# Moving the sums of batch 0 to VectorE, hT in two signs, and small writes to GpSimd in an attention kernel on one core

## The chip, the cores and the metric

The kernel runs on one core of a Trainium2 chip. The metric is the device time of one execution in microseconds (us). Engines are named as in the profile: PE is TensorE (PEld its weight loads), DVE is VectorE, ACT is ScalarE, POOL is GpSimd, SP is SyncE.

## What is computed

Two small networks one after the other. With x of 4 batches x 12544 rows x 128, and 32 inducing rows:

```python
def mab(q, kv):
    s = scale * (q @ kv.transpose(0, 2, 1))
    s = s - s.max(-1, keepdims=True)
    a = np.exp(s)
    a /= a.sum(-1, keepdims=True) + 1e-09
    return a @ kv
h = mab(I, x)            # 32 x 128 for each batch
y = mab(x, h)            # 12544 x 128 for each batch
...
h1 = y @ w1              # 128 x 1024
h2 = y @ w2
g = np.maximum(h1, h2)
return (g @ w_out)       # 1024 x 128
```

The kernel uses max(h1, h2) = relu(h2 - h1) + h1. So the output is relu(e (h (w2 - w1))) w_out + e (h w1 w_out), divided by the sums of e, where e are the exponentials of the second attention.

## The kernel before, in words

**Head: first attention of batch 0.** The x of batch 0 comes in 11 parts of 14, 7, 6, 5 or 3 slabs (a slab is 128 rows). Part 0 is loaded over SyncE's queue as fp32 and cast; parts 1 to 10 are loaded by GpSimd's queue with a cast to fp16 (load_x, L165). After them in the same queue come w1, w2 and w_out (L210 to L212), a memset of the tile m1bd (L219), seven loads of batch 1 (L165), and the four fp32 loads of weights_1 (L516, L517). For each part, p1_transpose has TensorE transpose the slabs (L232) and VectorE (L236) and ScalarE (L239) copy the result; p1_scores multiplies them with the inducing rows (L248) and ScalarE takes exponentials, et (L257); p1_accum has TensorE form the sums of et (L271, one column each) and the 32 x 128 sum h (L280). Between them, L657 and L665 are matmuls that compute nothing (fill).

**Ramp.** small_h scales h into hT (L423) and copies the sums (L433). weights_2 transposes w1 (L530). small_sums spreads the sums over the partitions with one fp32 matmul (L449) and takes the reciprocals rs and rw (L453, L454). stage computes e for a block of tokens (L591 on TensorE, L603 on ScalarE). small_hwd computes hwd = h (w2 - w1) (L469 and L470; copies at L477 and L484). weights_3 computes w1 w_out (L543, L551). small_m1 computes m1 = h w1 w_out (L493) and writes it to m1 and, as a diagonal block, to m1bd (L500 for batch 0, L504 for batch 3).

**Main loop.** A phase is four row-tiled matmul groups, e times hwd (L990, or m1 times e); ScalarE (L1006) and VectorE (L1009) take the relu of it out of PSUM. Output matmuls multiply the relu with w_out (L809). The first group of batch 0 and the last block of batch 3 are finished instead by a matmul with m1bd (L786). VectorE then divides by the sums of e (L836) and SyncE writes the output (L861). SyncE's queue also holds the DMA transposes of the next batch's x (L171). L766 are matmuls that compute nothing, put where the planner expects TensorE to wait.

**What sets the order.** All five engines are scheduled by hand: each engine's instruction order is the order in which the Python program emits them. The program decides what to emit next with a clock of its own (class Clock: expected times of TensorE, ScalarE, VectorE and of each of the eight PSUM banks; there is none for GpSimd) and with a table DEV, which tells for certain steps of the loop to deviate from the rule.

The program between the head and the loop ends like this:

```python
phase(plan_phase(False))
weights_3()
phase(plan_phase(False))
pending.append((small_m1, (0,)))
state["stage"] = 2
weights_1b()
```

weights_1b (L522) has GpSimd subtract the fp32 weights of weights_1 for the later batches (w21, first read at 92.8 us). small_m1 waits in the list pending and is emitted in the loop that follows.

Of the kernel before, what the change touches and what calls it, by code (L numbers as in the profile page):

```python
# [102 lines left out]
def kernel(  # L103
# [24 lines left out]
    etp = ctx.enter_context(tc.tile_pool(name="etp", bufs=3))  # L128
# [10 lines left out]
    ck = Clock()  # L139
    uid = [0]  # L140
# [37 lines left out]
    ones32 = consts.tile([128, 128], F32, name="ones32")  # L178
# [13 lines left out]
    rep32 = consts.tile([128, 128], F32, name="rep32")  # L192
# [4 lines left out]
    with tc.manual_schedule(engines={ET.PE, ET.DVE, ET.Activation, ET.Pool, ET.SP}):  # L197
# [5 lines left out]
        nc.sync.dma_start(ind_sb, inducing)  # L203
# [7 lines left out]
        nc.gpsimd.dma_start(out=w2h, in_=moe_w2)  # L211
# [3 lines left out]
        nc.vector.memset(ones32, 1.0)  # L215
# [7 lines left out]
        def p1_transpose(b, i, between=0):  # L223
# [3 lines left out]
            for g, m in ((0, h), (h, n - h)):  # L227
                if g and between:
                    fill(between)
                bi, ps = bank([128, 8, 128], F16)  # L230
                for j in range(m):
                    nc.tensor.transpose(ps[:, j, :], xn[:, g + j, :], identity16)  # L232
                end = ck.run(0.056 * m, ready=ck.bank[bi], why="T")
                dst = xT_tiles[b % 2][:, k0 + g : k0 + g + m, :]
                if g == 0:
                    nc.vector.tensor_copy(out=dst, in_=ps[:, 0:m, :])  # L236
                    ck.bank[bi] = ck.on_dve(end, 0.08 + 0.075 * m)
                else:
                    nc.scalar.copy(out=dst, in_=ps[:, 0:m, :])  # L239
                    ck.bank[bi] = ck.on_act(end, 0.05 + 0.12 * m)  # L240
                st[b]["xT", i] = max(ck.bank[bi], st[b].get(("xT", i), 0.0))
# [18 lines left out]

        def p1_accum(b, i, lo=0, hi=P1):
# [4 lines left out]
            if b == 0:  # L266
                last = i == len(parts[0]) - 1
                ck.wait(ready, "p1")
                for j in range(lo, hi, 4):
                    m = min(4, hi - j)  # L270
                    nc.tensor.matmul(  # L271
                        out=st[0]["eps"][0 : m * M, 0:1],
                        lhsT=et[:, j : j + m, :].rearrange("p k m -> p (k m)"),
                        rhs=ones16[:, 0:1],
                        start=(i == 0 and j == 0),
                        stop=(last and j + m == n),
                        skip_group_check=True,
                    )
# [8 lines left out]
                st[0]["end"] = ck.run(0.029 * (hi - lo) + 0.03 * ((hi - lo + 3) // 4))  # L287
# [130 lines left out]
        def small_h(b):  # L418
            hT4 = smp.tile([C, 4, M], F16, name=f"hT4_{b}", tag="hT4")
            if b == 0:  # L420


                nc.vector.tensor_scalar(  # L423
                    out=hT4,
                    in0=st[0]["hps"][:, None, 0:M].broadcast_to((C, 4, M)),
                    scalar1=DOWN,
# [3 lines left out]
                st[b]["hT4r"] = ck.on_dve(st[0]["end"], 0.3)  # L430
                ck.bank[st[0]["hb"]] = st[b]["hT4r"]
                es = smp.tile([128, 1], F32, name="es_0", tag="es")
                nc.scalar.copy(out=es, in_=st[0]["eps"][:, 0:1])  # L433
                ready = ck.on_act(st[0]["end"], 0.2)
                st[b]["hT4"] = hT4.rearrange("c q m -> c (q m)")
                return es, ready
# [8 lines left out]
        def small_sums(es, ready):  # L445

            ps = st[0]["eps"]
            ck.wait(ready, "p1")
            nc.tensor.matmul(out=ps[:, 2:3], lhsT=rep32, rhs=es, start=True, stop=True, skip_group_check=True)  # L449
            end = ck.run(0.11)  # L450
            st[0]["rs"] = smp.tile([128, 1], F32, name="rs_0", tag="rs_")
            st[0]["rw"] = smp.tile([128, 1], F32, name="rw_0", tag="rw_")
            nc.vector.reciprocal(out=st[0]["rs"], in_=ps[:, 2:3])  # L453
            nc.vector.tensor_scalar(out=st[0]["rw"], in0=st[0]["rs"], scalar1=1.0 / scale, scalar2=None, op0=ALU.mult)  # L454
            ck.bank[st[0]["eb"]] = st[0]["rsr"] = ck.on_dve(end, 0.34)

        def small_hwd(b, halves=(0, 1)):
            if 0 in halves:
                st[b]["hwd"] = smp.tile([128, J], F16, name=f"hwd_{b}", tag="hwd")
            hwd = st[b]["hwd"]  # L460
            for half in halves:
                for n in range(2 if b == 0 and half == 0 else 1):
# [5 lines left out]
                    if b == 0:  # L468
                        nc.tensor.matmul(out=ps, lhsT=st[b]["hT4"], rhs=w2h[:, sl], start=True, stop=False)  # L469
                        nc.tensor.matmul(out=ps, lhsT=st[b]["hT4"], rhs=w1h[:, sl], start=False, stop=True)  # L470
# [4 lines left out]
                    if half == 0 and n == 0:  # L475
# [14 lines left out]
        def small_m1(b):  # L490
            bi, ps = bank([128, 512])
            ck.wait(max(ck.bank[bi], st[b]["hT4r"]), "p1")
# [4 lines left out]
            outs = [(m1bd[32 * q : 32 * (q + 1), q, :], slice(32 * q, 32 * (q + 1))) for q in bd]  # L497
            for o, r in outs + [(m1, slice(0, 128))]:
                if b == 0:
                    nc.vector.tensor_scalar(  # L500
                        out=o, in0=ps[r, 0:128], scalar1=st[0]["rw"][r, :], scalar2=None, op0=ALU.mult
                    )
                else:
                    nc.vector.tensor_copy(out=o, in_=ps[r, 0:128])  # L504
                ck.bank[bi] = ck.on_dve(end, 0.2)
# [3 lines left out]
        w_of = {}  # L509

# [13 lines left out]
        def weights_2():  # L524
            for g in range(2):
                bi, ps = bank([128, 4, 128], F16)
                ck.wait(ck.bank[bi], "w")
# [3 lines left out]
                end = ck.run(0.056 * 4)  # L531
                if g == 0:
                    nc.vector.tensor_copy(out=w1T[:, 0:4, :], in_=ps)
                    ck.bank[bi] = ck.on_dve(end, 0.4)
                else:
                    nc.scalar.copy(out=w1T[:, 4:8, :], in_=ps)
                    ck.bank[bi] = w_of["w1T"] = ck.on_act(end, 0.5)

        def weights_3():
            bi, ps = bank([128, 512])  # L540
            ck.wait(max(ck.bank[bi], w_of["w1T"]), "w")
# [9 lines left out]
            nc.scalar.mul(out=w1out, in_=ps[:, 0:128], mul=-1.0)  # L551
            ck.bank[bi] = w_of["w1out"] = ck.on_act(end, 0.2)
# [73 lines left out]
        def dens(blk):  # L626
# [6 lines left out]
            bi, ps = bank([128, 512])  # L633
            ck.wait(ck.bank[bi], "den bank")
# [17 lines left out]
            ck.bank[bi] = ck.on_dve(end, 0.18 + 0.001 * 4 * n)  # L652
# [16 lines left out]
        for i in range(4):  # L669
            p1_transpose(0, i, 2 if i == 0 else 0)  # L670
            if i < 3:
                fill(2 - i // 2)
            if i == 0:
                bi, ps = bank([128, 512])
                nc.tensor.transpose(ps[:, 0:M], ind_sb, identity32[0:M, 0:M])
                nc.vector.tensor_copy(out=inducingT, in_=ps[:, 0:M])
                ck.bank[bi] = 0.0
                nc.vector.reduce_sum(out=diag, in_=identity32.rearrange("p (k m) -> p m k", m=M), axis=AX.X)
                for dst, f in ((rep32, DOWN / scale), (repd, 1.0)):
                    nc.vector.tensor_scalar(  # L680
                        out=dst.rearrange("p (k m) -> p k m", m=M),
                        in0=diag[:, None, :].broadcast_to((128, 4, M)),
                        scalar1=f,
                        scalar2=None,
                        op0=ALU.mult,
                    )
            if i > 0:
                p1_accum(0, i - 1)
            p1_scores(0, i)
        last = len(parts[0]) - 1  # L690
        p1_transpose(0, 4)
        p1_accum(0, 3)
        p1_transpose(0, 5)
        p1_scores(0, 4)
        for i in range(6, last + 1):
            p1_transpose(0, i)
            p1_scores(0, i - 1)
            p1_accum(0, i - 2)
        p1_scores(0, last)
        p1_accum(0, last - 1)  # L700
        p1_accum(0, last)
        for i in range(7):
            load_x(1, i)
        weights_1()
        nc.vector.tensor_scalar(out=w1h, in0=w1h, scalar1=-1.0, scalar2=None, op0=ALU.mult)
        sums = small_h(0)
        weights_2()
        small_sums(*sums)
        stage(blocks[0])
        small_hwd(0, (0,))  # L710
# [26 lines left out]
        def final_ready():  # L737
# [14 lines left out]
            return r  # L752
# [25 lines left out]
        def linear_last(end):  # L778

            while held:  # L780
                g = held[0]
                if g.full:
                    if st[g.blk.b].get("m1r", INF) > ck.pe:
# [102 lines left out]
        def want_linear():  # L886
# [7 lines left out]
            if st[g.blk.b].get("m1r", 0.0) > ck.pe + 0.2:  # L894
# [7 lines left out]
            22: 2, 33: 2, 78: 1, 95: 1, 97: 1, 103: 1, 104: 1, 106: 4, 116: 1, 118: 1, 119: 1, 125: 1, 127:  # L902
            2, 130: 1, 133: 1, 149: 2, 155: 1, 157: 4, 172: 1, 200: 1, 219: 1, 256: 2, 268: 1, 276: 3, 285:
            2, 297: 1, 324: 1, 327: 1, 339: 1, 344: 1, 357: 1, 368: 1, 399: 1, 466: 1, 478: 4, 481: 1, 484:
            1, 497: 1, 510: 2, 564: 1, 580: 1, 616: 2, 638: 1, 674: 4, 679: 1, 688: 1, 700: 3, 725: 2, 771:
            1, 784: 2, 795: 1, 830: 1, 832: 1, 838: 3, 839: 1, 847: 2, 855: 4, 932: 2, 958: 1, 962: 1, 969:
            1, 974: 1, 979: 1, 981: 1, 1041: 3, 1075: 1, 1102: 1, 1141: 4, 1154: 1, 1162: 2, 1168: 4, 1174:
            1, 1181: 2, 1207: 2, 1241: 1, 1247: 1, 1254: 1, 1258: 1, 1295: 1, 1331: 3, 1332: 3, 1343: 4,
            1365: 2, 1367: 1, 1380: 1, 1386: 1, 1390: 4, 1407: 4, 1411: 4, 1413: 3, 1420: 1, 1434: 1, 1442:
# [295 lines left out]
```

## Time and profile before

| what | us |
|---|---|
| median of 3 runs | 327.37 (327.37 to 327.51) |
| span of the profiled execution, first to last instruction | 325.6 |
| around the span (median less span) | 1.77 |
| first phase (L990) starts | 24.29 |
| first matmul with m1bd (L786) starts | 29.75 |
| m1bd written by VectorE (L500) | 27.38, takes 0.25 |
| subtractions of the weights by GpSimd (L522) | 41.11 and 42.54, 1.27 each |
| first output written out (L861) | 31.10 |

The profiled execution's own whole time is not recorded apart from the runs; its span is set against their median. A row of a timeline has the start, the length from the first start to the last end, engine, line, operation, out<-in and the count; in brackets the idle time of the engine before it and what ended that. A row of the chain has start, length and work. Matmul ends in the profile are modelled, so a busy TensorE is not one at its peak. The matmuls that compute nothing count as busy.

### The profile page before, as it was taken

Reading aid. Unit: us, or ns where it says so; the run is one execution under the profiler, and the core shown is the slowest. Engines: PE = TensorE matmul, PEld = TensorE weight load, DVE = VectorE, ACT = ScalarE, POOL = GpSimd, SP = SyncE. Lnnn points to the kernel's source line nnn. Section 1 sums busy time; section 2 is a strip of 40 time slices with the busy share of each in tenths; the row PEclk is TensorE's granted clock in tenths of the full one; section 3 lists DMA queues with packets and bytes.
Section 4 is the critical chain, followed back from the end, with each engine's and each line's share of the span. In section 5 each row is a group of like instructions: output and inputs, shape, how many; then the busy total and the mean of one; then the engine's idle time right before and its main releaser. Section 6 shows DMA issues by size and latency. Waiting matters only on the chain.

```text
span 325.6 us, 12570 instructions
## 1 busy us (share of the span) xinstructions
PE 319.8 (98%) x5404; PEld 243.0 (75%) x5404; DVE 283.1 (87%) x509; ACT 281.7 (87%) x560; POOL 25.6 (8%) x51
## 2 busy tenths in 40 slices
PE   7999999999999999999999999999999999999996
PEld 3876777777767777777777777777777777778785
DVE  3359989989989998998989999998989999999973
ACT  3679899999989899998888999989969999999961
POOL 7452030000040000000040000000000000000000
PEclk9999999999999999999999999999999999999999
DMA  8999999976279999993389999992312312222233
GB/s 204 208 206 214 286 246 212 172 207 134 97 150 245 225 248 209 201 203 86 116 162 243 214 234 232 190 192 86 115 66 101 113 68 98 90 108 99 85 115 112
DMA packets 70823, 53.65 MB, mean 165 GB/s; under 512 B 52176, under 2 KB 55408, under 8 KB 70768
## 3 DMA queue, kind: packets, MB, share of 16 engines
q1 hardware_dynamic: 64656, 38.63, 49.2%
q0 software_dynamic: 6112, 14.22, 22.3%
q8 instruction: 42, 0.69, 0.9%
q14 instruction: 13, 0.11, 0.1%
HBM read 28.33 MB, written 25.69 MB: 166 GB/s over the span
## 4 chain that ended last, share of the span: by engine, by line
PE 95%; DVE 1%; DMA 1%; ACT 0%; issue 0%; ACTq 0%; DVEq 0%
PE ps L809 61%; PE ps L990 22%; PE ps L591 2%; PE ps L232 2%; PE ps L308 2%; PE ps L364 1%; DMA xf<-in_x_dram 1%; PE ps L248 1%; DVE relu L1009 1%; PE ps L280 1%; PE ps L641 1%; PE ps L766 1%; PE ps L271 1%; PE ps L657 0%; PE ps L473 0%; PE ps L409 0%
## 5 line engine op out<-in xcount | busy, mean ns | idle before, releaser
L1006 ACT ACTIVATE relu<-ps 128x512 f16<-128x512 f32 x461 | 244.8, 602 | 26.6 <-PE ps L990 18.1
L1009 DVE TENSOR_SCALAR relu<-ps 128x512 f16<-128x512 f32 x323 | 206.8, 682 | 16.9 <-PE ps L990 15.3
L809 PE MATMUL ps<-woutp,relu 128*128 128x128 f16 x3136 | 217.3, 220 | 0.0
L809 PEld LDWEIGHTS <-relu 128*128 128x128 f16 x3136 | 176.7, 98 | 39.6 <-issue 29.1
L990 PE MATMUL ps<-e,hwd 32*128 32x512 f16 (+2 forms) x880 | 88.7, 360 | 0.0
L836 DVE TENSOR_TENSOR o<-ps,rp 128x512 f32<-128x512 f32 (+3 forms) x108 | 68.5, 634 | 5.5 <-PE ps L809 3.4
L990 PEld LDWEIGHTS <-hwd 32*128 32x128 f16 x880 | 24.9, 91 | 21.1 <-issue 1.0
L990 PE MATMUL ps<-m,e 32*128 32x128 f16 x381 | 38.8, 217 | 0.0
L990 PEld LDWEIGHTS <-e 32*128 32x128 f16 x381 | 21.3, 93 | 2.6
L165 POOL DMA_DIRECT2D xn<-in_x_dram x31 | 17.0, 557 | 8.2 <-DMA xn<-in_x_dram 4.3
L236 DVE COPY xT<-ps 128x512 f16<-128x512 f16 (+3 forms) x11 | 5.5, 504 | 7.8 <-PE ps L232 7.7
L319 ACT ACTIVATE eu<-ps 128x512 f16<-128x512 f32 x18 | 10.8, 615 | 0.0
L603 ACT ACTIVATE e<-ps 128x512 f16<-128x512 f32 (+2 forms) x21 | 10.5, 577 | 0.0
L164 POOL COPY pace<-hacc 128x1 f32<-128x1 f32 x2 | 0.4, 184 | 114.8 <-DVE hacc L397 114.8
L591 PE MATMUL ps<-xT,hT 128*32 128x512 f16 (+3 forms) x114 | 8.9, 362 | 0.0
L239 ACT COPY xT<-ps 128x768 f16<-128x768 f16 (+3 forms) x11 | 6.1, 556 | 2.7 <-PE ps L232 2.6
L232 PE MATMUL ps<-identity,xn 128*128 128x128 f16 x98 | 7.4, 219 | 0.4 <-DVE xn L661 0.3
L232 PEld LDWEIGHTS <-xn 128*128 128x128 f16 x98 | 5.6, 97 | 1.6 <-DVE xn L661 1.1
L257 ACT ACTIVATE et<-ps 128x448 f16<-128x448 f32 (+4 forms) x11 | 4.5, 413 | 2.6 <-PE ps L248 2.6
L308 PE MATMUL ps<-xT,inducingT 128*32 128x512 f16 x72 | 6.5, 385 | 0.0
L591 PEld LDWEIGHTS <-hT 128*32 128x32 f16 x114 | 3.3, 94 | 4.1 <-issue 3.0
L364 PE MATMUL ps<-xn,eT 128*32 128x128 f16 x288 | 5.5, 220 | 0.0
(96 smaller groups left out, 108.2 us busy)
## 6 DMA issues: line engine op xcount, KB each, us to landing
out_dram<-o SPq DMA_DIRECT2D x90, 256.0 KB, 2.4
xn<-in_x_dram POOLq DMA_DIRECT2D x24, 448.0 KB, 11.8
out_dram<-o SPq DMA_DIRECT2D x10, 128.0 KB, 3.0
xn<-in_moe_w_dram POOLq DMA_DIRECT2D x4, 256.0 KB, 14.1
xn<-in_x_dram POOLq DMA_DIRECT2D x4, 224.0 KB, 10.2
xT<-xn SPq DMA_TRANSPOSE x42, 4.3
xf<-in_x_dram SPq DMA_DIRECT2D x1, 512.0 KB, 3.9
xf<-in_x_dram SPq DMA_DIRECT2D x1, 384.0 KB, 4.3
```

The costliest lines, as they stand in the source:

```text
L165: nc.gpsimd.dma_start(out=xn_at[b, i][:, 0:n, :], in_=xr[b, :, k0 : k0 + n, :])
L232: nc.tensor.transpose(ps[:, j, :], xn[:, g + j, :], identity16)
L308: nc.tensor.matmul(out=ps[32 * g : 32 * (g + 1), :], lhsT=inducingT, rhs=xT_tiles[b % 2][:, U * u + 4 * g : U * u + 4 * (g + 1), :], start ...
L319: nc.scalar.activation(out=eu, in_=ps, func=AF.Exp, scale=scale, accum_out=st[b]["es"][:, u : u + 1])
L364: nc.tensor.matmul(out=ps[32 * g : 32 * (g + 1), 0:128], lhsT=eT[:, j, 32 * g : 32 * (g + 1)], rhs=xn_of(b, U * v + 4 * g + j), start=(j = ...
L591: nc.tensor.matmul(out=ps[32 * q : 32 * (q + 1), 128 * t : 128 * (t + n)], lhsT=hq, rhs=xT[:, c : c + n, :], start=True, stop=True, tile_p ...
L603: nc.scalar.activation(out=blk.e2[:, 0 : 128 * wd], in_=ps[:, 0 : 128 * wd], func=AF.Exp, scale=st[0]["rs"] if blk.b == 0 else scale,)
L809: nc.tensor.matmul(out=g.ps[:, 128 * c : 128 * (c + 1)], lhsT=g.blk.relu[q][:, 128 * (jb * w4 + t) : 128 * (jb * w4 + t + 1)], rhs=woutp[: ...
L836: nc.vector.tensor_mul(osb[:, 0:n, :], g.ps[:, 0 : n * C].rearrange("p (s c) -> p s c", s=n), rp)
L990: nc.tensor.matmul(**seq[i])
L1006: nc.scalar.activation(out=dst, in_=src, func=AF.Relu)
L1009: nc.vector.tensor_scalar(out=dst, in0=src, scalar1=0.0, scalar2=None, op0=ALU.max)
```

## The change

- The one-column matmuls of p1_accum (L271) go. A new function p1_sum has VectorE reduce et over the slabs of each part, add the parts up, and repeat the last sum four times; small_sums multiplies that with a column of the constant DOWN in one fp32 matmul. et gets four buffers instead of three.
- hT is copied by ScalarE, and a negated copy by VectorE; w1 is no longer negated. The product with w1 reads the negated copy. w1 w_out is copied without a sign.
- Both 256-column pieces of hwd are copied by VectorE; the first comes before the first stage, the second behind it.
- m1bd is no longer written by VectorE from PSUM: GpSimd copies it from m1.
- inducing is loaded over ScalarE's queue and transposed before x; w2 comes in two halves; one fill matmul less at two places; the order of the parts' steps changes; three small results share a PSUM bank (misc).
- The planner's clock starts at 1.2 us, knows when loads land (LANDED), and two entries of DEV differ. w1 w_out stands behind the first phase in the instruction order of both kernels.

The core of the diff:

```diff
-        nc.sync.dma_start(ind_sb, inducing)
+        nc.scalar.dma_start(ind_sb, inducing)
...
-        nc.gpsimd.dma_start(out=w2h, in_=moe_w2)
+        for h in range(2):
+            sl = slice(512 * h, 512 * (h + 1))
+            nc.gpsimd.dma_start(out=w2h[:, sl], in_=moe_w2[:, sl])
...
+        def p1_sum(i):
+            k0, n = parts[0][i]
+            et, ready = st[0]["et", i]
+            part = esum
+            if i > 0:
+                part = smp.tile([128, M], F32, name=f"esum_{i}", tag="esp")
+            nc.vector.reduce_sum(out=part, in_=et[:, 0:n, :].rearrange("p k m -> p m k"), axis=AX.X)
+            st[0]["sum"] = ck.on_dve(ready, 0.08 + n * M / 960.0)
+            if i == len(parts[0]) - 1:
+                nc.vector.tensor_add(
+                    out=esum4,
+                    in0=esum[:, None, :].broadcast_to((128, 4, M)),
+                    in1=part[:, None, :].broadcast_to((128, 4, M)),
+                )
+                st[0]["sum"] = ck.on_dve(0.0, 0.2)
+            elif i > 0:
+                nc.vector.tensor_add(out=esum, in0=part, in1=esum)
+                ck.on_dve(0.0, 0.1)
...
-                for j in range(lo, hi, 4):
-                    m = min(4, hi - j)
-                    nc.tensor.matmul(
-                        out=st[0]["eps"][0 : m * M, 0:1],
-                        lhsT=et[:, j : j + m, :].rearrange("p k m -> p (k m)"),
-                        rhs=ones16[:, 0:1],
...
+                nc.scalar.activation(
+                    out=hT4,
+                    in_=st[0]["hps"][:, None, 0:M].broadcast_to((C, 4, M)),
+                    func=AF.Copy,
+                    scale=DOWN,
+                )
...
+                neg = smp.tile([C, 4, M], F16, name="hT4n_0", tag="hT4n")
                 nc.vector.tensor_scalar(
-                    out=hT4,
+                    out=neg,
                     in0=st[0]["hps"][:, None, 0:M].broadcast_to((C, 4, M)),
-                    scalar1=DOWN,
+                    scalar1=-DOWN,
...
-            nc.tensor.matmul(out=ps[:, 2:3], lhsT=rep32, rhs=es, start=True, stop=True, skip_group_check=True)
+            nc.tensor.matmul(
+                out=ps[:, 0:1], lhsT=esum4.rearrange("p q m -> p (q m)"), rhs=down32, start=True, stop=True
+            )
...
         def small_m1(b):
-            bi, ps = bank([128, 512])
+            bi, ps = misc(256) if b == 0 else bank([128, 512])
...
-            outs = [(m1bd[32 * q : 32 * (q + 1), q, :], slice(32 * q, 32 * (q + 1))) for q in bd]
-            for o, r in outs + [(m1, slice(0, 128))]:
-                if b == 0:
-                    nc.vector.tensor_scalar(
-                        out=o, in0=ps[r, 0:128], scalar1=st[0]["rw"][r, :], scalar2=None, op0=ALU.mult
-                    )
-                else:
-                    nc.vector.tensor_copy(out=o, in_=ps[r, 0:128])
-                ck.bank[bi] = ck.on_dve(end, 0.2)
+            if b == 0:
+                nc.vector.tensor_scalar(out=m1, in0=ps[:, 0:128], scalar1=st[0]["rw"], scalar2=None, op0=ALU.mult)
+            else:
+                nc.vector.tensor_copy(out=m1, in_=ps[:, 0:128])
+            ck.bank[bi] = ck.on_dve(end, 0.2)
+            for q in bd:
+                r = slice(32 * q, 32 * (q + 1))
+                nc.gpsimd.tensor_copy(out=m1bd[r, q, :], in_=m1[r, :])
+            st[b]["m1bdr"] = ck.bank[bi] + 0.5 + 0.3 * len(bd)
...
+        def misc(lo):
+            if "misc" not in w_of:
+                w_of["misc"] = bank([128, 512])
+                ck.wait(ck.bank[w_of["misc"][0]], "misc")
+                ck.bank[w_of["misc"][0]] = INF
+            bi, ps = w_of["misc"]
+            return bi, ps[:, lo : lo + 128]
...
-            nc.scalar.mul(out=w1out, in_=ps[:, 0:128], mul=-1.0)
+            nc.scalar.copy(out=w1out, in_=ps[:, 0:128])
...
         last = len(parts[0]) - 1
...
+        for i in range(2, last):
+            if i > 2:
+                p1_sum(i - 3)
             p1_transpose(0, i)
             p1_scores(0, i - 1)
-            p1_accum(0, i - 2)
+            if i < last - 1:
+                p1_accum(0, i - 2)
...
-        nc.vector.tensor_scalar(out=w1h, in0=w1h, scalar1=-1.0, scalar2=None, op0=ALU.mult)
-        sums = small_h(0)
+        small_h(0)
         weights_2()
-        small_sums(*sums)
+        small_sums()
+        small_hwd(0, (0,), (0,))
         stage(blocks[0])
-        small_hwd(0, (0,))
+        small_hwd(0, (0,), (1,))
...
                 if g.full:
-                    if st[g.blk.b].get("m1r", INF) > ck.pe:
+                    if st[g.blk.b].get("m1bdr", INF) > ck.pe:
                         return
...
         phase(plan_phase(False))
-        weights_3()
+        blocks[0].staged = max(blocks[0].staged, st[0]["hwdr"])
+        weights_3(0)
         phase(plan_phase(False))
```

## The prediction

> **What bounds the kernel.** I read the page first (busy shares, slices, chain), then the timelines of TensorE and GpSimd for 0 to 45 us, then the waits.
>
> ```profile
> PE 319.8 (98%) x5404; PEld 243.0 (75%) x5404; DVE 283.1 (87%) x509; ACT 281.7 (87%) x560; POOL 25.6 (8%) x51
> ...
> PE 95%; DVE 1%; DMA 1%; ACT 0%; issue 0%; ACTq 0%; DVEq 0%
> ```
>
> TensorE is busy for 98% of the span, and 95% of the chain that ended last is TensorE's own work. So a microsecond that TensorE loses anywhere after the ramp is a microsecond of the result, unless something later gives it back. GpSimd looks free (8%), which is the trap in this case: the share says nothing of how long its queue stands still.
>
> The ramp ends near 29.7 us. From there the chain in order of time is TensorE piece after TensorE piece without a gap:
>
> ```profile
> 29.72 0.19 PE ps L809
> 29.91 0.06 PE ps L786
> 29.96 0.56 PE ps L809 x10
> 30.52 0.28 PE ps L990 x3
> 30.80 0.71 PE ps L809 x10
> ```
>
> L786 is the matmul that finishes the first output group; its moving operand is m1bd. In the timeline of TensorE it starts at 29.75 us. Now the timeline of GpSimd (start, length, what; in brackets the idle time before it and what ended it):
>
> ```profile
> 14.52 0.89 POOL L212 DMA_DIRECT2D woutp<-in_moe_w_out_dram  x1 [0.57 <-DMA xn<-in_x_dram]
> 15.40 0.54 POOL L219 MEMSET m1bd<- 128x512 f16 x1
> ...
> 26.14 0.54 POOL L517 DMA_DIRECT2D xn<-in_moe_w_dram  x1 [1.61 <-PE ps L641]
> 28.34 0.54 POOL L516 DMA_DIRECT2D xn<-in_moe_w_dram  x1 [1.66 <-DMA xn<-in_x_dram]
> 30.45 0.54 POOL L517 DMA_DIRECT2D xn<-in_moe_w_dram  x1 [1.57 <-PE ps L786]
> 41.11 1.27 POOL L522 TENSOR_TENSOR w<-xn,xn 128x512 f16<-128x512 f32 x1 [10.12 <-DMA xn<-in_moe_w_dram]
> 42.54 1.27 POOL L522 TENSOR_TENSOR w<-xn,xn 128x512 f16<-128x512 f32 x1 [0.15 <-DMA xn<-in_moe_w_dram]
> ```
>
> The two L522 are weights_1b's subtractions w2 - w1. GpSimd stands 10.12 us before the first, because the four fp32 weight loads are behind seven loads of batch 1, and is through with them at 42.54 + 1.27 = 43.81 us. In this kernel nobody cares: w21 is first read at 92.8 us.
>
> **The change, part by part.**
>
> *m1bd on GpSimd (the part that decides).* VectorE wrote the block of m1bd at 27.38 (L500, 0.25 us) straight from PSUM. In the changed kernel GpSimd copies it from m1. small_m1 runs inside the main loop, and weights_1b() is called ahead of that loop, so in GpSimd's instruction order the copy stands right behind both subtractions: load, load, load, load, subtract, subtract, copy to m1bd. TensorE's order still has the m1bd matmul after the fifth phase, with a wait on GpSimd in front of it. So a wait is added, and what is queued behind it is all the rest of TensorE's program. VectorE's next output (the first L836, at 30.80) needs that matmul, and SyncE's first output and all its transposes (31.10, 34.83 and on) stand behind that output. No engine can feed TensorE in the meantime.
>
> Does GpSimd keep its order? The memset of m1bd above waits for nothing, and still ran only at 15.40, behind five DMA issues that GpSimd stood waiting to make, for 0.97, 1.62, 1.67, 0.54 and 0.57 us from 7.0 on. It doesn't let a ready instruction pass a waiting one.
>
> When is the copy done? Upper figure: the subtractions as now, to 43.81; a gap of 0.1; the copy, 32x128, between the 0.18 of the 128x1 copy (L164) and the 0.54 of the 128x512 memset: I take 0.3; TensorE starts 0.07 after its releaser (VectorE's first cast ends at 5.31, the transposes start at 5.38). That is 44.3. Lower figure: SyncE's outputs and transposes between 31 and 42.5 us won't be there. The issues at 26.14, 28.34, 30.45 each wait for one more landing of a 448 KB load, so the queue alone lands one in 2.15 us. Four more from 30.45 make 39.05 in issue times, less 0.3 between a landing and the issue behind it, 38.75; the four weight loads at 1.43 a pair (42.54 - 41.11) end at 41.6; subtraction 42.9, copy and signal 43.35. Splitting w2 adds one DMA to the queue for the same bytes, so I allow 0.1 and take **43.5**, near the lower end because the competing transfers are surely gone. Delay of the m1bd matmul against now: 43.5 - 29.75 = **13.75 us**, bounds 13.6 and 14.55.
>
> *TensorE after the standstill.* The only place in this trace where TensorE comes out of idleness is the start:
>
> ```profile
> 1.19 3.85 PE L665 MATMUL ps<-warm 128*128 128x512 f16 x9 [1.19 <-DVE warm L213]
> ...
> 5.83 0.60 PE L657 MATMUL ps<-warm 128*128 128x512 f16 x2
> ```
>
> Nine 128x512 matmuls take 3.85 us, 0.43 each; the two at 5.83 take 0.45 together in the chain, 0.22 each. The granted clock reads 1.00 in both, so the page doesn't show it. If 13 us of idleness bring that state back, 9 x 0.21 = **1.9 us** more are lost (0 if they don't; 2.1 if the half rate lasted to the first transposes: (5.38 - 1.19) / 2). TensorE has no slack afterwards to hide it. The row doesn't tell how long an idle time it needs; I take 1.9, from the one case there is.
>
> [...]
>
> *Sums of batch 0 by VectorE.* 29 one-column matmuls (L271) go, four in 0.27 us at 9.58: 29 x 0.066 = 1.9 us of TensorE between 9.6 and 21.6. VectorE gets 11 reductions, 9 adds and one broadcast add: the nearest row is the 128x128 reduction L678, 0.36, so 21 x 0.15 to 0.7, some 3 to 15 us, and I take 8, in a stretch where it is busy 2.4 of 5 us. The transposes of the last part of x start at 20.01, issued 10.16 and landed 9.3 later, at 19.5: at most 0.55 is to be won there. Against it, the last reductions, the broadcast add, the negated hT and the w1T copy (0.42) now stand in VectorE's queue before the reciprocal that the first exponentials need; that can cost as much as it wins.
>
> *hT plain and negated, weights, order.* The negation of w1h (0.43), one copy of es (0.16) and the diag scaling (0.28) go; the hT copy moves to ScalarE (a 128x128 there: L551, 0.30), the negated one to VectorE (0.29 now); the second 256-column hwd piece moves from ScalarE to VectorE (0.48). The fp32 sum matmul keeps its form (0.34). 14 instead of 16 fill matmuls of 512 columns, 12 instead of 13 of 256. inducing is loaded over ScalarE's queue, and its transpose now stands ahead of x's first: if it still landed at 1.66 + 5.2 = 6.9, the first transposes would slip 1.5 us. w1 times w_out stands behind the first phase in both instruction orders; only its PSUM bank and sign change. Three small results now share one bank.
>
> **All of this head is worth between -1.0 (0.55, and the 0.43 of the negation, which now stands between the last copies and hT) and +2.0 us (the slip of 1.5, and 0.5 in VectorE's queue) at the first phase (24.29 now). I take -0.3, and none of it counts:** whatever it wins, TensorE then waits longer for the same copy, whose time comes from GpSimd's load queue; whatever it costs is covered up to 13 us. Without that cover it would be the whole result.
>
> *The rest.* After the m1bd matmul the two instruction orders of TensorE agree until about two thirds of the program, then phases and output matmuls change places with equal counts: -0.4 to +0.4, taken as 0. The last batch's four m1bd copies leave VectorE (4 x 0.29 at 242 to 243) for an idle GpSimd, and are needed near 320: nothing.
>
> **Sum.** Span 325.6, plus 1.77 around it, is the median 327.37. 325.6 + 13.75 + 1.9 = 341.25 span, **343.0 us**.
>
> **Rivals.** (a) The standstill without the half rate: 327.37 + 13.75 = 341.1. For it: no row shows an idle time in mid-run that brings it back; against: the start. 0.16. (b) No standstill: the copy runs before TensorE arrives at 29.75, so only the head counts, 327.37 - 0.3 = 327.1, from 326.4 (head 1 faster) to 329.4. It needs the copy past the subtractions, or the weights landed by 29.75 - 0.47 - 2 x 1.27 = 26.7 instead of 42.5; it decides once that margin of 16 us is gone. Against it stand the order, the 10.12 and the memset. 0.04: half of it faster, a quarter same, a quarter slower. (c) The loads land as late as now or later, 44.3 and beyond, with the half rate: 327.37 + 14.55 + 1.9 = 343.8 and up. 0.18. The forecast, resume at 43.3 to 43.9 with the half rate: 0.62.
>
> The range takes in (a) at its lower bound, 13.6, with 0.4 less from the reordering: 340.6. It takes in (c) with 0.2 more of half rate, 0.4 of reordering and 0.3 of later loads: 344.7. What a measurement of this kernel can tell from no change is about 0.2%, 0.65 us. Faster 0.02, same 0.01, slower 0.97.
>
> **What would show it.** Right: GpSimd's m1bd copy right after the second subtraction, near 43 us; TensorE idle from about 29.5 to 43.5, put down to GpSimd; no output before 43; the first 128x128 matmuls after it at 0.11 instead of 0.056 for some 4 us (wrong about the half rate if at 0.056 at once). Wrong altogether: a copy before 30 us. Wrong in size: subtractions before 41 or after 43 us.

## The result and the profile after

The changed kernel takes 342.58 us (median of 5 runs, 342.17 to 343.17) against 327.48 for the kernel before: 1.0464 times as long, interval 1.0451 to 1.0476. The forecast was 343.0. The span is 340.6 us, 15.0 more than before.

On the page of the changed kernel, the busy shares, the slices of TensorE and its granted clock, and the chain by engine:

```profile
PE 321.6 (94%) x5372; PEld 243.1 (71%) x5372; DVE 290.0 (85%) x525; ACT 281.4 (83%) x558; POOL 27.3 (8%) x57
...
PE   8878099999999999999999999999999999999996
...
PEclk9989679999999999999999999999999999999999
...
PE 87%; DMA 6%; DVE 3%; POOL 1%; issue 1%; POOLq 0%
```

GpSimd still shows 8%. The fifth slice of TensorE (34 to 42.6 us) is a 0, and the clock is below full speed in two places: around 25 us and around 37 to 47 us (the digits 8, and 6 and 7; by windows it is 0.50 from 23.5 to 26.9 and from 37.1 to 47.4). Loads have grown from 1% to 6% of the chain (4% of it the fp32 weight loads), and GpSimd has come into it. The timelines of GpSimd and of TensorE in the changed kernel:

```profile
30.40 0.54 POOL L552 DMA_DIRECT2D xn<-in_moe_w_dram  x1 [1.62 <-PE ps L846]
40.00 2.51 POOL L557 TENSOR_TENSOR w<-xn,xn 128x512 f16<-128x512 f32 x2 [9.06 <-DMA xn<-in_moe_w_dram]
42.45 0.28 POOL L531 COPY m1bd<-m 32x128 f16<-32x128 f16 x1
```

```profile
32.89 0.23 PE L846 MATMUL ps<-woutp,relu 128*128 128x128 f16 x1
42.78 0.27 PE L823 MATMUL ps<-m1bd,e 128*128 128x128 f16 x1 [9.66 <-POOL m1bd L531]
42.84 1.16 PE L846 MATMUL ps<-woutp,relu 128*128 128x128 f16 x9
...
44.48 1.35 PE L846 MATMUL ps<-woutp,relu 128*128 128x128 f16 x11
...
47.97 0.96 PE L846 MATMUL ps<-woutp,relu 128*128 128x128 f16 x14
```

The m1bd copy stands right behind both subtractions, and TensorE idles 9.66 us for it. After it nine and eleven output matmuls need 1.16 and 1.35 us, and from 47.97 on fourteen need 0.96. The same stretches by window (length, then busy time of TensorE, its weight loads, VectorE, ScalarE, GpSimd; then granted clock, DMA share, GB/s):

```profile
33.00:36.00 3.00, 0.12 (x1) 0.00 (x0) 1.09 (x2) 1.06 (x3) 0.00 (x0) 1.00 1.08 214
36.00:40.00 4.00, 0.00 (x0) 0.00 (x0) 0.00 (x0) 0.00 (x0) 0.00 (x1) 0.64 0.94 313
...
44.00:46.00 2.00, 2.00 (x24) 1.50 (x24) 1.12 (x2) 1.08 (x2) 0.00 (x0) 0.50 0.11 33
...
48.00:50.00 2.00, 2.00 (x35) 1.57 (x31) 1.90 (x4) 1.88 (x5) 0.00 (x0) 1.00 0.05 12
```

**Where the 15.0 us came from.** Three landmarks, that is, instructions that both programs share, cut the span into stretches that can be compared: the m1bd matmul, the first and the last product with w21. The m1bd matmul before the change, and the products with w21 (w in the profile; first and last start) before and after it:

```profile
29.75 0.22 PE L786 MATMUL ps<-m1bd,e 128*128 128x128 f16 x1
...
L473 PE MATMUL ps<-w,hT x6: 379/380/391, 92.8 to 241.1; 128*128 128x512 f16 x6
...
L499 PE MATMUL ps<-w,hT x6: 379/379/389, 107.7 to 256.0; 128*128 128x512 f16 x6
```

| us | before | changed | difference |
|---|---|---|---|
| first phase starts | 24.29 | 27.10 | +2.8 |
| TensorE done ahead of the m1bd matmul | 29.75 | 33.1 | +3.4 |
| m1bd matmul starts | 29.75 | 42.78 | +13.0 |
| from it to the first product with w21 | 63.0 | 64.9 | +1.9 |
| from the first to the last product with w21 | 148.3 | 148.3 | 0 |
| from the last one to the end | 84.5 | 84.6 | +0.1 |

So 13.0 of standstill and 1.9 behind it, while the clock is at half, are the result. The late head is inside the 13.0: it only made the idle time 9.7 us long instead of 13. Landmarks come from one profiled run of each kernel. Kernels with the same head differ by 0.3 to 0.7 us in them (the first phase starts at 24.29 before the change and at 23.85 in e3, at 27.10 in the changed kernel, 27.44 in e1 and 27.78 in e4), so smaller differences between two heads tell nothing.

### The profile page after: what moved, and what is told of

Same layout as the page of the kernel before. It is cut to its first block, busy times and chain, and to the rows that moved or that the text cites. A ratio compares the mean times of both kernels' runs of the same rounds, so it can differ in the third digit from the quotient of the medians.

```text
span 340.6 us, 12526 instructions
## 1 busy us (share of the span) xinstructions
PE 321.6 (94%) x5372; PEld 243.1 (71%) x5372; DVE 290.0 (85%) x525; ACT 281.4 (83%) x558; POOL 27.3 (8%) x57
## 3 DMA queue, kind: packets, MB, share of 16 engines
q1 hardware_dynamic: 64608, 38.62, 47.4%
## 4 chain that ended last, share of the span: by engine, by line
PE 87%; DMA 6%; DVE 3%; POOL 1%; issue 1%; POOLq 0%
PE ps L846 59%; PE ps L1028 21%; DMA xn<-in_moe_w_dram 4%; DMA xn<-in_x_dram 2%; PE ps L627 2%; DVE esum L275 2%; PE ps L325 1%; PE ps L381 1%; DVE xT L243 1%; PE ps L677 1%; POOL w L557 1%; DVE esum L285 1%; PE ps L499 0%; PE ps L426 0%; POOL xn L168 0%
## 5 line engine op out<-in xcount | busy, mean ns | idle before, releaser
L336 ACT ACTIVATE eu<-ps 128x512 f16<-128x512 f32 x18 | 10.8, 614 | 0.0
L823 PE MATMUL ps<-m1bd,e 128*128 128x128 f16 x11 | 1.5, 223 | 9.7 <-POOL m1bd L531 9.7
L531 POOL COPY m1bd<-m 32x128 f16<-32x128 f16 x5 | 1.4, 285 | 75.5 <-DVE m L527 75.3
L275 DVE TENSOR_REDUCE esum<-et 128x32 f32<-128x448 f16 (+4 forms) x11 | 6.9, 626 | 0.0
## 6 DMA issues: line engine op xcount, KB each, us to landing
xn<-in_x_dram POOLq DMA_DIRECT2D x4, 224.0 KB, 10.2
```

The source lines that it names most:

```text
L275: nc.vector.reduce_sum(out=part, in_=et[:, 0:n, :].rearrange("p k m -> p m k"), axis=AX.X)
L336: nc.scalar.activation(out=eu, in_=ps, func=AF.Exp, scale=scale, accum_out=st[b]["es"][:, u : u + 1])
```

## The experiments

The theory: GpSimd's place in the queue costs 13 us, the clock 2, and a head that is over 3 us late is hidden behind them. Rivals: the loss is elsewhere in the change; the copy is dear on GpSimd wherever it stands; the clock shown costs nothing; the head is a gain. Ratios are to the kernel before, measured on the same chip.

**e1: m1bd by VectorE, nothing else.**

```diff
-                nc.gpsimd.tensor_copy(out=m1bd[r, q, :], in_=m1[r, :])
+                nc.vector.tensor_copy(out=m1bd[r, q, :], in_=m1[r, :])
```

> The changed kernel with the m1bd copies on VectorE instead of GpSimd, nothing else. Theory (the standstill behind GpSimd's two subtractions is the whole loss, and it hides a head that came out 3.2 us late: TensorE reached the m1bd matmul at 33.0 us instead of 29.75): no idle time at that matmul, no lower clock after it, 342.6 - 9.7 - 2.2 = about 330.6 us. Rival 1 (the head is a small gain, as the prediction had it): 327.1. Rival 2 (the loss comes from something else in the change): above 335.

Measured 331.86 us, 1.0127 (1.0111 to 1.0142). TensorE doesn't wait at the m1bd matmul:

```profile
33.30 0.22 PE L823 MATMUL ps<-m1bd,e 128*128 128x128 f16 x1
```

One line is worth 3.4% (1.0464 less 1.0127); what is left is a loss, so the rival of a gaining head falls. It is 1.3 us more than expected: on this chip the kernel before took 327.82, 0.3 more than in the result, the head of this run was 0.3 later, and the end is 0.3 to 0.4 longer (below, e9 to e12).

**e2: the copy ahead of the subtractions, still on GpSimd.**

```diff
             st[b]["m1"] = m1
             st[b]["m1r"] = ck.bank[bi]
+            if b == 0:
+                weights_1b()
...
-        weights_1b()
```

> The changed kernel with the two subtractions emitted behind GpSimd's copy of m1bd instead of ahead of it; the copy stays on GpSimd. Theory (the place in the queue costs, not the engine): the copy runs near 31 us, TensorE doesn't wait, the same 330.6 us as with VectorE's copy, within 0.5. Rival (a copy on GpSimd is slow or late by itself): more than 1 us above that.

331.28 us, 1.0105 (1.0090 to 1.0120): no worse than VectorE. The copy on GpSimd:

```profile
31.54 0.28 POOL L531 COPY m1bd<-m 32x128 f16<-32x128 f16 x1
```

TensorE takes the m1bd matmul at 33.42 without a wait. The engine isn't the fault, the queue is.

**e3: the kernel before, with the copy on GpSimd alone.**

```diff
-            outs = [(m1bd[32 * q : 32 * (q + 1), q, :], slice(32 * q, 32 * (q + 1))) for q in bd]
+            outs = []
             for o, r in outs + [(m1, slice(0, 128))]:
...
+            for q in bd:
+                r = slice(32 * q, 32 * (q + 1))
+                nc.gpsimd.tensor_copy(out=m1bd[r, q, :], in_=m1[r, :])
```

> The kernel before with one part of the change alone: m1bd is copied from m1 by GpSimd, behind the subtractions. TensorE reaches the m1bd matmul at 29.75 instead of 33.0. Theory (the end of the wait is set by GpSimd's loads alone, so an earlier head wins nothing): resume at 42.8, 342.5 us, the same as the whole change within 0.5. Rival (the head's 3.2 us count beside the standstill): 342.6 - 3.2 = 339.4 us.

342.54 us, 1.0456 (1.0436 to 1.0476). One line makes the whole loss, whatever the head does. TensorE's timeline in e3:

```profile
42.81 0.26 PE L790 MATMUL ps<-m1bd,e 128*128 128x128 f16 x1 [13.34 <-POOL m1bd L508]
```

TensorE arrived 3.6 us earlier than in the changed kernel and stood 3.7 us longer.

**e4: TensorE kept busy during the standstill.**

```diff
+                    if g.blk.b == 0:
+                        for _ in range(42):
+                            nc.tensor.matmul(
+                                out=g.ps, lhsT=warm[:, 0:128], rhs=warm, start=False, stop=False, skip_group_check=True
+                            )
```

> The changed kernel with 42 matmuls that compute nothing (zeros added) in front of the first m1bd matmul, 42 x 0.216 = 9.1 us in the 9.7 us that TensorE idles. Theory (2 us of the loss are the half clock after the standstill): the granted clock stays at 1.00 from 33 us on, the copy still ends near 42.7, and the time falls to 340.6 us. Rival (the clock shown costs nothing): 342.6. If the fill delays the matmul: 342.6 or more with no idle time at it.

341.19 us, 1.0413 (1.0396 to 1.0431), 0.6 above the 340.6 expected. The profiled run's copy ended 0.4 later, and the m1bd matmul came at 43.22, but the way from it to the first product with w21 is 63.0 us as before, not 64.9. In the windows of e4 the clock stays up:

```profile
42.00:44.00 2.00, 1.94 (x22) 1.08 (x20) 0.29 (x1) 0.00 (x0) 1.16 (x2) 1.00 0.00 0
44.00:46.00 2.00, 2.00 (x36) 1.41 (x31) 1.65 (x4) 1.71 (x4) 0.00 (x0) 1.00 0.15 41
```

36 matmuls instead of 24 from 44 to 46 us: the clock costs 1.9 us there, and work that computes nothing buys it back.

**The head.** e1 leaves 1.3% unexplained. In the changed kernel VectorE's timeline near the end of the head shows no idle time:

```profile
15.96 0.90 DVE L275 TENSOR_REDUCE esum<-et 128x32 f32<-128x448 f16 x1
16.90 0.19 DVE L285 TENSOR_TENSOR esum<-esum,esum 128x32 f32<-128x32 f32 x1
17.01 0.42 DVE L243 COPY xT<-ps 128x512 f16<-128x512 f16 x1
17.34 0.53 DVE L275 TENSOR_REDUCE esum<-et 128x32 f32<-128x224 f16 x1
17.90 0.19 DVE L285 TENSOR_TENSOR esum<-esum,esum 128x32 f32<-128x32 f32 x1
18.01 0.42 DVE L243 COPY xT<-ps 128x512 f16<-128x512 f16 x1
```

It is busy 10.46 of the 10.8 us from 12.6 to 23.4 (4.84 before), and the copies of xT, for which TensorE's scores wait (0.17, 0.28 and 0.43 us at 19.49, 20.43 and 21.30), stand behind the sums. TensorE has gaps, and its clock falls to 0.50 from 23.5 to 26.9 us. There is a second wait:

```profile
23.49 0.59 PE L566 MATMUL ps<-identity,w1h 128*128 128x128 f16 x4 [1.15 <-DVE w1T L569]
```

The new weights_2 asks for both PSUM banks before it marks the first as taken, so both halves of the transposed w1 get the same bank. e5 to e8 start from e2.

**e5: two banks.** Edit in weights_2, after the choice of the bank:

```diff
+                ck.bank[bi] = INF
```

> The kernel of e2 (copy first), and in weights_2 the bank of the first four transposes of w1 marked as taken until their copy, so that the second four get another PSUM bank. In the changed kernel the second four waited 1.15 us for VectorE's copy of the first four. Theory (the head's loss is mostly VectorE's queue, and this wait is a part of it): TensorE's sum matmul is then held by VectorE's last add (22.9 us) instead of 23.9, 0.9 us earlier; 330.4 us, against 331.3 for e2. If the wait is the main cause of the 3.3 us that the head lost: 329 or less. If it is hidden: 331.3.

330.78 us, 1.0091 (1.0062 to 1.0121), near the 330.4 expected. But the interval overlaps that of e2: alone, this is not shown to matter.

**e6: sums of parts 1 to 9 left out**, with one bank as changed.

```diff
         def p1_sum(i):
+            if 0 < i < len(parts[0]) - 1:
+                return
```

> The kernel of e2 without the reductions and adds of parts 1 to 9 on VectorE (only the first and the last part are summed, so the sums of batch 0 are left out in the main). Theory (VectorE is the bound of the head: from 12.6 to 23.4 us its queue has no gap): the copies of xT come earlier, TensorE stands less and keeps its full clock from 23 to 27 us; 2 to 3 us less than e2, 328.3 to 329.3. Rival (the reductions lie beside other work): within 0.5 of e2's 331.3.

329.98 us, 1.0070 (1.0052 to 1.0087): 0.35% less than e2, or 1.1 us, where 2 to 3 were expected. The wait for the one bank is still there (0.79 us).

**e7: both edits.**

> e5 and e6 together: two banks in weights_2, and the sums of parts 1 to 9 left out. If both causes add: 327.5 to 328.3. If the reductions alone were the cause, the same as e6.

329.86 us, 1.0072 (1.0050 to 1.0095): a miss of 1.6 us. The first phase started at 23.51, earlier than before the change, and then TensorE's timeline has

```profile
31.74 0.22 PE L828 MATMUL ps<-m1bd,e 128*128 128x128 f16 x1 [2.22 <-POOL m1bd L533]
```

while in the windows of e7 the clock falls after it:

```profile
31.00:32.00 1.00, 0.26 (x5) 0.26 (x5) 0.01 (x1) 0.00 (x0) 0.69 (x2) 1.00 1.10 219
32.00:33.00 1.00, 1.00 (x15) 0.52 (x12) 0.29 (x1) 0.00 (x0) 0.00 (x0) 0.62 1.03 204
33.00:34.00 1.00, 1.00 (x13) 0.99 (x11) 0.82 (x2) 0.90 (x2) 0.00 (x0) 0.50 1.08 215
```

GpSimd's timeline tells why TensorE waits:

```profile
30.85 0.54 POOL L556 DMA_DIRECT2D xn<-in_moe_w_dram  x1 [1.62 <-DVE relu L1052]
31.39 0.30 POOL L533 COPY m1bd<-m 32x128 f16<-32x128 f16 x1
```

Ahead of the subtractions the copy still stood behind the issue of the last weight load, for which GpSimd idles 1.62 us until 30.85; the chain of e7 has the landing of an earlier load (to 30.31) ahead of that issue. e2 hid this: its TensorE came too late to notice (the copy was done at 31.82, the m1bd matmul started at 33.42). The half clock doesn't come in every run: the profiled run and one other (mean clock 0.995) took 331.21 and 330.99 us, the other three (0.999 to 1.000) 329.31 to 329.86. So the median has the wait without the half clock, and the half clock costs some 1.5 us where it comes.

**e8: a whole kernel, sums back on TensorE** (the one-column matmuls of p1_accum and the fp32 spread as before the change; two banks; copy first).

> A whole kernel: the changed one with the copy first, two banks in weights_2, and the sums of batch 0 back on TensorE (29 one-column matmuls, the spread by one fp32 matmul as before; the copy of the sums on VectorE). What is left of the change: hT in two signs, the loads, the order of the parts, the small copies. Theory (the sums on VectorE are the bad part, the rest is a small gain): 326.6 to 327.6 us, at or a little under the kernel before. Rival (TensorE's 1.9 us of sums cost what VectorE's did): 329 or more.

329.52 us, 1.0060 (1.0045 to 1.0076), a miss of 1.9 us. TensorE's timeline has

```profile
24.02 0.40 PE L623 MATMUL ps<-xT,hT 128*32 128x512 f16 x4 [0.96 <-PE ps L489]
...
31.69 0.22 PE L820 MATMUL ps<-m1bd,e 128*128 128x128 f16 x1 [0.23 <-POOL m1bd L524]
```

The m1bd matmul ran right behind GpSimd's copy, as in e7, but that cost only 0.23 us. Most of the loss is earlier: the first phase starts at 25.43, 1.1 us later than before, with 0.96 us of idle time for which the profile names no other engine, and the way from there to the m1bd matmul takes 6.3 us (5.5 before, 4.4 in e11).

**e9 to e12: m1bd on VectorE.** e9 is e7 with that, and with the subtractions in their place of the changed kernel. e10 and e12 give each of the three small results a bank of its own:

```diff
         def misc(lo):
-            if "misc" not in w_of:
-                w_of["misc"] = bank([128, 512])
...
+            bi, ps = bank([128, 512])
+            ck.wait(ck.bank[bi], "misc")
```

e10 is e9 with that; e11 is e10 with the sums on TensorE; e12 is e10 with all sums on VectorE, so the whole change mended.

> The kernel of e7 (two banks in weights_2, sums of parts 1 to 9 left out) with m1bd written by VectorE. In e7 the head was 0.8 us earlier than before (first phase 23.5 against 24.3), but TensorE stood 2.2 us at the m1bd matmul and ran at half clock after it: GpSimd's copy, though ahead of the subtractions, was still behind the issue of the last weight load at 30.85. Theory: without GpSimd in the way the matmul runs at 29.5 and the clock stays up, 329.9 - 2.2 - 0.6 to 1 = 326.7 to 327.1 us. Rival (e7's time comes from the head): 329.9.

> The kernel of e9, and the three small results (sums of e, w1 w_out, m1) in PSUM banks of their own, as before the change. In e7 TensorE waited 0.6 us for ScalarE's copy of w1 w_out and then for the reciprocal, both readers of the shared bank. Theory: these waits go, 0.5 to 0.9 us less than e9, about 326.2. Rival (other waits take their place): the same as e9. The order of TensorE's next 200 matmuls changes a little with it.

> A whole kernel: sums of batch 0 on TensorE, two banks in weights_2, banks of their own for the small results, m1bd on VectorE; the rest as changed. e8, which was held by GpSimd's copy at 31.7, without that. Theory: the head is about as long as before and nothing waits for GpSimd, 326.8 to 327.8 us, equal to the kernel before within 0.2%. If the rest of the change (loads, hT in two signs, order of the parts) is a gain: under 326.8.

> The whole change with its three waits mended: m1bd on VectorE, two banks in weights_2, banks of their own for the small results; the sums stay on VectorE. e5 was 330.8 with the m1bd matmul at 33.0. Theory (the sums on VectorE keep the head late, and nothing else is left): 329.8 to 330.3 us, still about 2.5 us above before. Rival (the three waits were all of it): 327.5 or less.

| | e9 | e10 | e11 | e12 |
|---|---|---|---|---|
| sums of batch 0 | left out in the main | left out in the main | TensorE | VectorE |
| first phase, us | 23.46 | 23.44 | 24.27 | 25.88 |
| m1bd matmul | 29.3 | 27.9 | 28.7 | 30.6 |
| first product with w21 (before: 92.8) | 92.4 | 92.2 | 93.0 | 95.3 |
| median | 327.65 | 327.50 | 327.92 | 330.47 |
| ratio | 1.0007 (0.9998 to 1.0015) | 1.0005 (0.9996 to 1.0013) | 1.0014 (1.0006 to 1.0023) | 1.0092 (1.0079 to 1.0106) |

- e12 less e10 is the price of the sums of parts 1 to 9 on VectorE with everything else mended: 0.87%, 2.9 us. e11 less e10 is the price of having all sums on TensorE instead: 0.09%, 0.3 us, and the intervals overlap.
- A part of the 2.9 is the half clock of the head, which comes and goes here too: the one run of e12 with a mean clock of 1.000 took 329.35 us, the four at 0.994 and 0.995 took 330.24 to 330.56, the one at 0.990 331.18. By that one run, 1.9 us are the queue of VectorE and 1.1 the clock.
- e12 less e1 is what two banks and own banks bring together, without the sums being touched: 0.35%, 1.1 us.
- The own banks alone (e10 against e9) bring nothing that can be told, against the expectation: the m1bd matmul comes 1.5 us earlier, but the first product with w21 only 0.2.
- e9's head is 0.83 us shorter than before, and the total isn't (expected 326.7 to 327.1). At the first product with w21 0.4 is left, which is within the difference between two runs. From 28 to 34 us VectorE and ScalarE are busy all the time in e9, as they are before the change:

```profile
28.00:30.00 2.00, 2.00 (x32) 1.34 (x29) 2.00 (x5) 2.00 (x5) 0.54 (x1) 1.00 1.06 210
30.00:32.00 2.00, 2.00 (x34) 1.39 (x34) 2.00 (x5) 1.99 (x5) 0.54 (x1) 1.00 1.06 210
```

The ramp then seems to be bound also by taking the relu out of PSUM; that a part of the 0.83 is lost there was read from the trace, not tested. Another 0.4 goes at the end: from the last product with w21 it is 84.9 us in e1 and e9 to e12, and 84.5 or 84.6 in all others. The four copies for batch 3, which these kernels give to VectorE without a place in the planner's clock, are the edit that they share; that they cost it is not shown. GpSimd for those four and VectorE for batch 0 was not tried. No version beat the kernel before.

## Why the prediction was right, point by point

- **The standstill: right in cause, mis-sized, 13.0 against 13.75.** Cause, place and what is queued behind were as told; e1, e2 and e3 show that it is the queue position alone. But 13.0 lies below the lower bound, 13.6, and subtractions before 41 us were my own sign of a wrong size. The term that was mis-sized is the loads. Both subtractions ran back to back from 40.00 (2.51 us). By the prediction's sum the first pair of loads lands at 40.2, which fits, but the second at 41.6, and the second subtraction waits for it: the 1.43 taken there for the loading of a pair is the distance of the two subtractions, which holds the 1.27 of the first one. In the changed kernel the second subtraction waits for no load. The prediction also allowed 0.1 for the split of w2. The copy took 0.28 (0.3).
- **The half clock: right, 1.9 against 1.9** (e4). That an idle time in mid-run brings the half rate was an estimate from the one row of the trace where TensorE leaves an idle time, the start; no row of before shows it in mid-run. In the changed kernel TensorE stops at 33.1 us and the granted clock reads 0.50 from 37.1 on; in e4, with TensorE kept busy, it stays at 1.00 from 30 to 50 us. That the sizes agree to the tenth is luck. TensorE ran at half from 42.78 to about 47.4, 4.6 us, and lost less than half of that. In e3, after the same standstill, it was at half for only 3.5 us, and the way from the m1bd matmul to the first product with w21 took 64.5 us, so that the loss was 1.4.
- **The head: wrong, hidden.** Forecast -0.3 within -1.0 and +2.0, measured +2.8 at the first phase. The step that failed is "that can cost as much as it wins". The price was about right (8 us taken; 8.9 measured: 6.9 of reductions, 1.7 of adds and 0.3 for the last one), but I set it against VectorE's share of busy time, not against its queue: the sums stand between the copies that TensorE waits for. I also missed the shared bank of weights_2 and the fall of the clock to 0.50, for 3.4 us, that came behind TensorE's gaps.
- **"None of it counts": right.** e3 has the head of before and the time of the whole change.
- **The rest at 0: right.** 148.3 us in both, and +0.1 in the last third, in spite of the changed order there.
- **Rivals.** (a) would have been 341.1, and e4 shows that about this is left without the half clock (341.19). (b) fell, but its own number was wrong: without the standstill the change is 331.9, not 327.1. (c) fell: the loads landed earlier (a median of 13.0 us from issue to landing for the weights, 14.1 before).

## What to carry to other kernels

An engine at 8% busy can still be the worst place for a small write (0.28 us of copy, 13.0 us of delay here): read what its queue waits for at that moment, and put the write ahead of the waiting instructions or on another engine. A planner without a clock for GpSimd can't see such a wait; an order written by hand needs one for each queue that it emits to. Where a large wait is added, mend it before judging the rest of a change: here it hid a head some 3 us late, and in e7 a smaller wait of the same kind hid a head that was earlier than before. Look also at the clock of every run: where it falls in some runs only, as in e7 and e12, a median mixes two kinds of runs.

## What the runs showed of the hardware that was not expected

TensorE's clock fell to half without a long idle time. Worked out from the granted clock by windows, the halved stretches are 23.5 to 26.9 us in the changed kernel's head, 32.2 to 35.7 in the profiled run of e7, and 37.1 to 47.4 around the standstill: 3.4, 3.4 and 10.2 us, one, one and three times 3.4. In the 3.4 us ahead of the first, TensorE was busy for 1.35 us, 40%, and never idle for more than 1.15 us at a time; ahead of the second it was idle for 2.2 us. Much busier stretches went before such a fall too: in e6 and in e12 the clock is at half for 3.4 us from 24.0 on, and in the 3.4 us ahead TensorE was busy for some 2.47 and 2.35 us by the windows, 73% and 69%. In e8, with 0.96 us of idleness at 23 us, the share is as low as 70% (2.37 of 3.40 us from 20.6), and the clock stayed at 1.00. So no busy share can be named from which on it falls, and by e7 and e12 the same kernel falls in one run and not in another (mean clocks 0.995, and 0.999 to 1.000, in e7; 0.990 to 0.995, and 1.000, in e12).

At the very start nine 128x512 matmuls run at 0.43 us each while the granted clock reads 1.00; the 42 of the same shape in e4 take 9.23 us, 0.22 each, at the same reading. After the standstill half rate reads 0.50 (24 matmuls from 44 to 46 us, 36 in e4 at 1.00). So at the start the column doesn't show the half rate.

A reduction on VectorE over the outer index (128x448 fp16 to 128x32) took 0.90 to 0.93 us, where the copy of 128x512 fp16 out of PSUM took 0.42.

What stays open: why TensorE stood 0.96 us before the first stage in e8, with no other engine named, and what decides in which runs the clock falls.
